# A decode block on one Trainium2 core: the K chunks of a head as an inner loop of two turns, and x's columns in 16 loads

## The chip, the core and the metric

The kernel runs on one core of one Trainium2 chip. The core has a matrix engine (TensorE, PE in the profile; PEld is its weight load), a vector engine (VectorE, DVE), a scalar engine (ScalarE, ACT), GpSimd (POOL) and a sync engine (SyncE, SP). They run separate instruction streams and meet at semaphores. Sixteen DMA engines move data between HBM and the on-chip memory SBUF; in this kernel loads are issued by SP and by ACT, each on a queue of its own (q1 and q10 in the profile). TensorE writes to the banks of PSUM. The metric is the device time of one execution in microseconds, lower is better.

## The reference, cut to what matters

One token goes through layernorm, grouped-query attention over a cache of 65536 positions (8 KV heads, 4 query heads each, head size 128), a residual, a second layernorm and a bilinear gated feed-forward layer with its residual.

```python
q = (layernorm(x) @ wq).reshape(B, Sq, 32, 128)          # x is [1, 1, 512]
scores = einsum("bhqd,bhkd->bhqk", q, k) * (128 ** -0.5)  # k_cache, v_cache: [1, 8, 65536, 128]
o = einsum("bhqk,bhkd->bhqd", softmax(scores), v)
h = x + o.reshape(B, Sq, 4096) @ wo
n = layernorm(h)
out = h + ((n @ w_gate) * (n @ w_up)) @ w_down            # 512 -> 1792 -> 512
```

All data are float32. The two caches are 512 MiB together and are read once.

## The kernel before, in words

**Tiling.** Of each head, K is read in NT = 4 chunks and then V in 4 chunks. A chunk is a tile of 128 partitions x 16384 floats, 64 KB in a partition, 8 MiB in all. Two buffers, `kv[0]` and `kv[1]`, take the chunks in turn. The loads are `sp.dma_start` at line 148 (line 144 for the last V chunk of the last head, which comes in four pieces). Before each load but the first two, SP waits (line 133) until TensorE has finished the chunk that stood in the same buffer, by a count on TensorE's semaphore `pe`. A head's projection weights (`wqo`, lines 138 and 140) are loaded between V chunks. At the end come the weights of the feed-forward layer (lines 154 to 161).

**Start.** ACT issues the load of `x_col`, x as 128 partitions x 4 columns (line 125), then that of `x_row`, x as one row (line 126). SP issues the first head's query weights `wq_sb` (line 128) and the first two K chunks. VectorE sums `x_col` (line 185) after waiting for it at line 184; mean, variance and the normalised `xn` follow, with two small matmuls of TensorE (lines 327 and 330) and a square root on ACT (line 196) between. VectorE then makes small constants (lines 204 to 215) and copies `x_row` (line 218). All of this is in one order on VectorE, ahead of the first head's work.

**TensorE's loop over heads** (line 392, eight turns, code in `head()`). First 16 matmuls make the head's four queries (line 337); VectorE copies them into `q_pad` (line 228) and gives one count on the semaphore `tok`. Then, for each of the four K chunks, TensorE takes the chunk's load off `s_kv` and issues 32 matmuls (line 347) into PSUM bank `psc[s % 2]`. ACT copies the bank out (line 225), VectorE takes a maximum of the copy (line 231); the maxima of chunks 0 and 1 give a count on `tok` each, and chunks 2 and 3 take one before they overwrite the bank. The softmax follows (lines 353 to 365), then the matmuls over the V chunks (line 375) and the output projection (lines 382 and 388).

The loop exists for TensorE alone: the streams of the other engines are written out for all eight heads. `take(s, n)` waits until semaphore `s` has `n` and takes them off.

Of the kernel before, what the change touches and what calls it, by code (L numbers as in the profile page):

```python
# [26 lines left out]
HKV, REP, DH = 8, 4, 128  # L27
SK = 65536
CK = 16384
NT = SK // CK  # L30
# [8 lines left out]
PE_ONLY = bass.OrderedEngineSet([mybir.EngineType.PE])  # L39
# [20 lines left out]
def body(nc, xc, xr, kT, v, wq0, wqo, wo7, wg, wu, wd, out):  # L60
    pe_e, dve_e, act_e, pool_e, sp = nc.tensor, nc.vector, nc.scalar, nc.gpsimd, nc.sync

    def tile(name, *shape, align=32):
        return nc.alloc_sbuf_tensor(name, list(shape), F32, align_bytes=align).ap()

    def bank(name):
        return nc.alloc_psum_tensor(name, [P, 512], F32).ap()

    x_col, x_row = tile("x_col", P, KT), tile("x_row", 1, D)
# [4 lines left out]
    q_pad = tile("q_pad", P, 2 * 28 + REP)  # L74
# [6 lines left out]
    kv = [tile(f"kv{i}", P, CK, align=1024) for i in range(2)]  # L81
# [16 lines left out]
    psc = [bank(f"psc{i}") for i in range(2)]  # L98
    ptp = [bank(f"ptp{i}") for i in range(2)]
    pva, attn = bank("pva"), bank("attn")  # L100
    sm = [bank(f"sm{i}") for i in range(2)]
# [3 lines left out]
    def sem(name):  # L105
        sems.append(nc.alloc_semaphore(name))
        return sems[-1]

    pe, dve, act, pool = (Counter(sem(n)) for n in ("pe", "dve", "act", "pool"))
    tok, atok = sem("tok"), sem("atok")  # L110
    s_kv = [sem("s_kv0"), sem("s_kv1")]
# [5 lines left out]
    s_x, s_xr, s_out = sem("s_x"), sem("s_xr"), sem("s_out")  # L117
# [3 lines left out]
    def pe_at(h, m):  # L121
        return M_HEAD * h + m


    act_e.dma_start(x_col, xc).then_inc(s_x, 16)
    act_e.dma_start(x_row, xr).then_inc(s_xr, 16)

    sp.dma_start(wq_sb, wq0).then_inc(s_wq, 16)
# [45 lines left out]
    def dve_self():  # L174
        dve_e.wait_ge(dve.sem, dve.n)
# [5 lines left out]
    dve.tick(dve_e.memset(mean_m, 1.0 / D))  # L181
    dve.tick(dve_e.memset(ones, 1.0))
    dve.tick(dve_e.memset(eps_t, EPS))
    dve_e.wait_ge(s_x, 16)
    c_s1 = dve.tick(dve_e.tensor_reduce(out=ln_s, in_=x_col, axis=AX.X, op=ALU.add))
    dve_e.wait_ge(pre, PRE_PM)
    dve.tick(dve_e.tensor_copy(ln_m, sm[0][:, 0:1]))
# [33 lines left out]
    for h in range(HKV):  # L221
        copies = []
        for s in range(NT):
            act_e.wait_ge(pe.sem, pe_at(h, M_K + s))
            copies.append(act.tick(act_e.copy(sc[s], psc[s % 2])))  # L225

        dve_e.wait_ge(pe.sem, pe_at(h, M_Q))
        dve_e.tensor_copy(q_pad[:, 28:28 + REP], sm[0][:, 0:REP]).then_inc(tok, 1)
        for s in range(NT):
            dve_e.wait_ge(act.sem, copies[s])  # L230
            i = dve_e.tensor_reduce(out=mx[:, s:s + 1], in_=sc[s], axis=AX.X, op=ALU.max)  # L231
            if s < 2:

                i.then_inc(tok, 1)
            else:
                dve.tick(i)
        dve_self()
        dve_e.tensor_reduce(out=m1, in_=mx, axis=AX.X, op=ALU.max).then_inc(tok, 1)
        dve_e.wait_ge(pe.sem, pe_at(h, M_MX))
        dve.tick(dve_e.tensor_reduce(  # L240
            out=mrow, in_=sm[1][0:1, 0:P].rearrange("p (g h) -> p h g", h=REP), axis=AX.X, op=ALU.max))
        dve_self()
        dve_e.tensor_copy(mexp, mrow.unsqueeze(1).to_broadcast([1, 32, REP])).then_inc(tok, 1)
        dve_e.wait_ge(pe.sem, pe_at(h, M_MB))
        c_bias = dve.tick(dve_e.tensor_scalar(  # L245
            out=nbias, in0=sm[0][:, 0:1], scalar1=-SCALE, scalar2=None, op0=ALU.mult))

        act_e.wait_ge(dve.sem, c_bias)
        for s in range(NT):
            act_e.activation(  # L250
                sc[s], sc[s], AF.Exp, bias=nbias[:, 0:1], scale=SCALE,
                accum_out=sums[:, s:s + 1]).then_inc(atok, 1)
        for s in range(NT):
            dve_e.wait_ge(pe.sem, pe_at(h, M_T + s))
            dve_e.tensor_copy(  # L255
                pt[s].rearrange("p g b h -> p b g h"),
                ptp[s % 2].rearrange("p (b g h) -> p b g h", b=4, h=REP)).then_inc(tok, 1)
        dve.tick(dve_e.tensor_reduce(out=l1, in_=sums, axis=AX.X, op=ALU.add))
        dve_self()
        dve_e.tensor_scalar(  # L260
            out=l4, in0=sel_h, scalar1=l1[:, 0:1], scalar2=None, op0=ALU.mult).then_inc(tok, 1)
        dve_e.wait_ge(pe.sem, pe_at(h, M_L))
        dve.tick(dve_e.reciprocal(linv, sm[1][:, 0:REP]))
        dve_e.wait_ge(pe.sem, pe_at(h, M_V + NT - 1))
        dve_e.tensor_copy(orow, pva).then_inc(tok, 1)  # L265
        dve_self()
        dve_e.wait_ge(pe.sem, pe_at(h, M_PO))
        dve_e.tensor_tensor(
            out=o_pad[:, :, 0], in0=sm[0][:, 0:REP], in1=linv, op=ALU.mult).then_inc(tok, 1)
        if h < LAST:  # L270
            dve_e.wait_ge(dve.sem, c_acc)
            dve_e.wait_ge(pe.sem, pe_at(h, M_AT))
            c_acc = dve.tick(dve_e.tensor_tensor(out=acc, in0=attn, in1=acc, op=ALU.add))
# [47 lines left out]
    mm = pe_e.matmul  # L321

    def take(s, n=1):
        pe_e.wait_ge(s, n).then_inc(s, -n)  # L324
# [9 lines left out]
    def head():  # L334
        for r in range(REP):
            for k in range(KT):
                i = mm(sm[0][:, r:r + 1], wq_sb[:, k, r * P:(r + 1) * P], xn[:, k:k + 1],  # L337
                       start=(k == 0), stop=(k == KT - 1))
        i.then_inc(pe.sem, 1)
        take(tok)  # L340
        for s in range(NT):
            take(s_kv[s % 2], 16)
            if s >= 2:
                take(tok)
            for rs in range(8):
                for j in range(4):
                    i = mm(psc[s % 2][32 * j:32 * j + 32, :],  # L347
                           q_pad[:, 28 - 4 * rs:60 - 4 * rs],
                           kv[s % 2][:, (4 * rs + j) * 512:(4 * rs + j + 1) * 512],
                           start=(rs == 0), stop=(rs == 7))  # L350
            i.then_inc(pe.sem, 1)
        take(tok)
        pe_e.transpose(sm[1][0:1, 0:P], m1, ident).then_inc(pe.sem, 1)  # L353
        take(tok)
        mm(sm[0][:, 0:1], mexp.rearrange("p g h -> p (g h)"), ones[0:1, 0:1],  # L355
           start=True, stop=True).then_inc(pe.sem, 1)
        for s in range(NT):
            take(atok)
            if s >= 2:
                take(tok)  # L360
            for b in range(4):
                i = pe_e.transpose(ptp[s % 2][:, b * P:(b + 1) * P], sc[s][:, b * P:(b + 1) * P], ident)  # L362
            i.then_inc(pe.sem, 1)
        take(tok, 3)
        mm(sm[1][:, 0:REP], ones, l4, start=True, stop=True).then_inc(pe.sem, 1)  # L365
        for j in range(4):
            mm(pva[32 * j:32 * j + 32, :], zeros[:, 0:32], zeros, start=True, stop=False)  # L367
        for n in range(NT):
            vt = kv[n % 2]
            pieces = list(zip(V_CUTS, V_CUTS[1:])) if n == NT - 1 else [(0, 32)]  # L370
            for p, (lo, hi) in enumerate(pieces):
                take(s_vp[p] if len(pieces) > 1 else s_kv[n % 2], 16)
                for w in range(lo, hi):
                    rs, j = divmod(w, 4)
                    i = mm(pva[32 * j:32 * j + 16, :],  # L375
                           pt[n][:, 8 * j + rs, :, :].rearrange("p b h -> p (b h)"),
                           vt[:, w * 512:(w + 1) * 512],
                           start=False, stop=(n == NT - 1 and rs == 7))
            i.then_inc(pe.sem, 1)
        take(tok)  # L380
        for b in range(4):
            i = mm(sm[0][:, 0:REP], orow[:, b * P:(b + 1) * P], sel_b[:, 4 * b:4 * b + 4],  # L382
                   start=(b == 0), stop=(b == 3))
        i.then_inc(pe.sem, 1)
        take(s_w, 16)
        take(tok)
        for r in range(REP):
            i = mm(attn[32 * r:32 * r + 32, :], o_pad[:, r, :], wo_sb[:, r, :],  # L388
                   start=True, stop=True)
        i.then_inc(pe.sem, 1)  # L390

    with nc.Fori(0, HKV, engines=PE_ONLY, hint_back_edge=True):
        head()
# [27 lines left out]
    for b in range(2):  # L421
        i = mm(sm[0][:, 4 * b:4 * b + 4], f_sb[:, b * P:(b + 1) * P], sel_q,
               start=(b == 0), stop=(b == 1))
# [4 lines left out]
    for i in range(2):  # L428
        i2 = mm(sm[1][64 * i:64 * i + 64, 4:6], f_sb[:, 3 * P:FJ], sel_q[:, 2 * i:2 * i + 2],
                start=False, stop=True)  # L430
    i2.then_inc(pe.sem, 1)
    pe_e.wait_ge(dve.sem, c_fp0)
    for c in range(NC):
# [4 lines left out]
        for j in range(4):  # L438
            o = c * D + j * P
            i = mm(pva[32 * j:32 * j + 32, 0:P], f_pad[:, c, :], wd_t[:, o:o + P],  # L440
                   start=False, stop=(c == NC - 1))
# [43 lines left out]
```

## Time and profile before

| | |
|---|---|
| median of 3 runs | 1310.22 us (1310.11 to 1310.87) |
| the profiled execution | 1310.07 us, of which the span from first to last instruction 1308.8 us |
| bytes read from HBM | 564.66 MB |
| TensorE matmul busy | 711.7 us, 54% of the span |
| VectorE, ACT, GpSimd busy | 73.3, 47.2 and 2.5 us |
| DMA queue q1 (SP's loads) | 12248 packets, 564.67 MB |
| DMA queue q10 (ACT's loads) | 146 packets |

The page puts an engine's busy time next to the span; a share of the DMA queues is a share of the 16 DMA engines' time. The timeline view gives start and length in us from the span's start, the engine, the line, the operation and what it writes and reads; in brackets stand the engine's idle time before it and what ended that. An "SPq" or "ACTq" row is the issuing of a load by that engine's sequencer, not the transfer.

### The profile page before, as it was taken

How to read it: one execution, taken by the hardware profiler on the slowest of the kernel's cores; microseconds unless marked ns; L12 is line 12 of the kernel's file. 1: busy time of each engine (PE TensorE's matmuls, PEld its weight loads, DVE VectorE, ACT ScalarE, POOL GpSimd, SP SyncE). 2: the span in 40 equal slices, each digit the busy share in tenths (PEclk: the TensorE clock that was granted, in tenths of full speed). 3: DMA queues.
4: the chain of work that ended last, by engine and by line, in shares of the span. 5: the costliest groups of instructions: out<-in, count | busy, mean ns of one | idle time of the engine just before them, and what ended most of it. 6: DMA issues, size and time to landing. Idle time of an engine off the chain costs nothing. (4 is left out here: it accounts for less than half of the span.)

```text
span 1308.8 us, 10526 instructions
## 1 busy us (share of the span) xinstructions
PE 711.7 (54%) x4922; PEld 247.5 (19%) x4922; DVE 73.3 (6%) x180; ACT 47.2 (4%) x102; POOL 2.5 (0%) x13
## 2 busy tenths in 40 slices
PE   4366384553755446563564636636365465655556
PEld 3012031210312112120131202202021121311113
DVE  0000000100001000010000100001000010000101
ACT  0000000100001000010000100001000010000100
POOL 0000000000000000000000000000000000000000
PEclk9776666776767867767767867678677677687778
DMA  9999999999999999999999999999999999999998
GB/s 417 417 445 429 435 437 431 441 429 441 425 441 425 441 431 437 435 435 435 433 439 427 441 425 441 431 439 433 435 433 435 441 416 450 425 441 429 441 417 373
DMA packets 12404, 564.80 MB, mean 432 GB/s; under 512 B 1509, under 2 KB 1513, under 8 KB 2154
## 3 DMA queue, kind: packets, MB, share of 16 engines
q1 hardware_dynamic: 12248, 564.67, 99.7%
q8 instruction: 6, 0.10, 0.0%
q10 hardware_dynamic: 146, 0.00, 0.0%
q14 instruction: 4, 0.03, 0.0%
HBM read 564.66 MB, written 0.00 MB: 431 GB/s over the span
## 5 line engine op out<-in xcount | busy, mean ns | idle before, releaser
L347 PE MATMUL psc<-kv,q_pad 128*32 128x512 f32 x2048 | 295.2, 741 | 254.0 <-PEq L324 254.0
L375 PE MATMUL pva<-kv,pt 128*16 128x512 f32 x2048 | 280.6, 709 | 276.5 <-PEq L324 276.5
L347 PEld LDWEIGHTS psc<-kv,q_pad 128*32 128x32 f32 x2048 | 81.1, 133 | 461.6 <-issue 461.6
L375 PEld LDWEIGHTS pva<-kv,pt 128*16 128x16 f32 x2048 | 67.5, 111 | 492.4 <-issue 492.4
L225 ACT COPY sc<-psc 128x512 f32<-128x512 f32 x32 | 18.7, 585 | 1142.7 <-PE psc L347 1142.7
L231 DVE TENSOR_REDUCE mx<-sc 128x1 f32<-128x512 f32 x32 | 21.9, 686 | 536.6 <-ACT sc L225 536.6
L337 PEld LDWEIGHTS sm<-xn,wqo_sb 128*128 128x128 f32 x256 | 49.0, 299 | 10.3 <-issue 10.3
L337 PE MATMUL sm<-xn,wqo_sb 128*128 128x1 f32 x256 | 49.7, 329 | 2.2 <-issue 2.2
L265 DVE COPY orow<-pva 128x512 f32<-128x512 f32 x8 | 5.5, 692 | 566.9 <-PE pva L375 566.9
L362 PE MATMUL ptp<-ident,sc 128*128 128x128 f32 x128 | 29.3, 396 | 10.2 <-PEq L324 9.7
L362 PEld LDWEIGHTS ptp<-ident,sc 128*128 128x128 f32 x128 | 21.4, 202 | 15.5 <-issue 14.7
L250 ACT ACTIVATE sc<-sc,nbias 128x512 f32<-128x512 f32 x32 | 22.7, 711 | 20.2 <-DVE nbias L245 20.2
L255 DVE COPY pt<-ptp 128x512 f32<-128x512 f32 x32 | 22.1, 692 | 21.6 <-PE ptp L362 21.6
L367 PE MATMUL pva<-zeros 128*32 128x512 f32 x64 | 12.9, 890 | 0.0
L388 PE MATMUL attn<-wqo_sb,o_pad 128*32 128x512 f32 x64 | 10.8, 748 | 3.4 <-PEq L324 3.4
L382 PE MATMUL sm<-sel_b,orow 128*128 128x4 f32 x64 | 8.2, 252 | 7.2 <-PEq L324 7.2
L382 PEld LDWEIGHTS sm<-sel_b,orow 128*128 128x128 f32 x64 | 7.7, 191 | 14.4 <-issue 14.4
L353 PE MATMUL sm<-ident,m 128*1 128x128 f32 x8 | 2.2, 269 | 13.6 <-PEq L324 13.6
L410 PE MATMUL psc<-kv,hn_pad 128*32 128x448 f32 x64 | 8.2, 654 | 1.8 <-DMA kv<-in_wu 1.0
L365 PE MATMUL sm<-l,ones 128*128 128x4 f32 x16 | 3.9, 312 | 9.6 <-PEq L324 9.6
L355 PE MATMUL sm<-ones,mexp 1*128 1x1 f32 x16 | 3.3, 275 | 5.7 <-PEq L324 5.7
L250 ACT ACTIVATION_READ_ACCUMULATOR sc<-sc,nbias 128x1 f32 x32 | 6.0, 187 | 0.0
(83 smaller groups left out, 64.5 us busy)
## 6 DMA issues: line engine op xcount, KB each, us to landing
wqo_sb<-in_wqo SPq DMA_DIRECT2D x7, 2048.0 KB, 15.1
kv<-in_v SPq DMA_DIRECT2D x1, 4096.0 KB, 21.6
kv<-in_wg SPq DMA_DIRECT2D x1, 3584.0 KB, 18.8
kv<-in_v SPq DMA_DIRECT2D x1, 2048.0 KB, 26.1
kv<-in_v SPq DMA_DIRECT2D x2, 1024.0 KB, 29.1
kv<-in_wu SPq DMA_DIRECT2D x1, 1792.0 KB, 22.9
kv<-in_wu SPq DMA_DIRECT2D x2, 896.0 KB, 25.4
kv<-in_wd SPq DMA_DIRECT2D x1, 1536.0 KB, 19.7
```

Source lines behind the costliest of these rows:

```text
L225: copies.append(act.tick(act_e.copy(sc[s], psc[s % 2])))
L231: i = dve_e.tensor_reduce(out=mx[:, s:s + 1], in_=sc[s], axis=AX.X, op=ALU.max)
L250: act_e.activation(sc[s], sc[s], AF.Exp, bias=nbias[:, 0:1], scale=SCALE, accum_out=sums[:, s:s + 1]).then_inc(atok, 1)
L255: dve_e.tensor_copy(pt[s].rearrange("p g b h -> p b g h"), ptp[s % 2].rearrange("p (b g h) -> p b g h", b=4, h=REP)).then_inc(tok, 1)
L337: i = mm(sm[0][:, r:r + 1], wq_sb[:, k, r * P:(r + 1) * P], xn[:, k:k + 1], start=(k == 0), stop=(k == KT - 1))
L347: i = mm(psc[s % 2][32 * j:32 * j + 32, :], q_pad[:, 28 - 4 * rs:60 - 4 * rs], kv[s % 2][:, (4 * rs + j) * 512:(4 * rs + j + 1) * 512], st ...
L362: i = pe_e.transpose(ptp[s % 2][:, b * P:(b + 1) * P], sc[s][:, b * P:(b + 1) * P], ident)
L367: mm(pva[32 * j:32 * j + 32, :], zeros[:, 0:32], zeros, start=True, stop=False)
L375: i = mm(pva[32 * j:32 * j + 16, :], pt[n][:, 8 * j + rs, :, :].rearrange("p b h -> p (b h)"), vt[:, w * 512:(w + 1) * 512], start=False, ...
L382: i = mm(sm[0][:, 0:REP], orow[:, b * P:(b + 1) * P], sel_b[:, 4 * b:4 * b + 4], start=(b == 0), stop=(b == 3))
L388: i = mm(attn[32 * r:32 * r + 32, :], o_pad[:, r, :], wo_sb[:, r, :], start=True, stop=True)
L410: i = mm(acc[32 * j:32 * j + 32, :FJ], hn_pad[:, k, :], w[:, o:o + FJ], start=(k == 0), stop=(k == KT - 1))
```

## The change

Two things are edited.

**TensorE's K chunks.** The Python loop that wrote out four chunks becomes a hardware loop on TensorE of `NT // 2 = 2` turns inside the loop over heads, whose body holds two chunks, one for each buffer. As both turns run the same code, every chunk now takes a count of `tok`, the first two as well; VectorE's copy into `q_pad` therefore gives 3 counts in place of 1.

**x's columns.** The one load of 128 rows becomes 16 loads on ACT's queue, of 8, 1, 2, 3, ... and 15 rows (8 + 120 = 128). VectorE waits for all of them. The load of `x_row` is issued after them.

```diff
-    act_e.dma_start(x_col, xc).then_inc(s_x, 16)
+    at = 0
+    for r in (8, *range(1, 16)):
+        act_e.dma_start(x_col[at:at + r], xc[at:at + r]).then_inc(s_x, 16)
+        at += r
     act_e.dma_start(x_row, xr).then_inc(s_xr, 16)
...
-    dve_e.wait_ge(s_x, 16)
+    dve_e.wait_ge(s_x, 16 * 16)
...
-        dve_e.tensor_copy(q_pad[:, 28:28 + REP], sm[0][:, 0:REP]).then_inc(tok, 1)
+        dve_e.tensor_copy(q_pad[:, 28:28 + REP], sm[0][:, 0:REP]).then_inc(tok, 3)
...
-        for s in range(NT):
-            take(s_kv[s % 2], 16)
-            if s >= 2:
+        with nc.Fori(0, NT // 2, engines=PE_ONLY):
+            for s in range(2):
+                take(s_kv[s], 16)
                 take(tok)
-            for rs in range(8):
-                for j in range(4):
-                    i = mm(psc[s % 2][32 * j:32 * j + 32, :],
+                for rs in range(8):
+                    for j in range(4):
+                        i = mm(psc[s][32 * j:32 * j + 32, :],
...
-            i.then_inc(pe.sem, 1)
+                i.then_inc(pe.sem, 1)
```

ACT's stream at its start, the loads of x and the square root of the first layernorm; before:

```order
L125 DMA x_col<-in_xc 128x4 [waits barrier_Pool_Activation_PE_DVE_SP_release]
L126 DMA x_row<-in_xr 1x512
L196 ACT_TABLE_LOAD
L196 ACTIVATE ln_t<-sm,eps_t 128x1 [waits pre]
L225 COPY sc<-psc 128x512 [waits pe] x4
```

And now, the last eight of the 16 loads and what follows them (the lines are those of the changed file):

```order
L128 DMA x_col<-in_xc 8x4
L128 DMA x_col<-in_xc 9x4
L128 DMA x_col<-in_xc 10x4
L128 DMA x_col<-in_xc 11x4
L128 DMA x_col<-in_xc 12x4
L128 DMA x_col<-in_xc 13x4
L128 DMA x_col<-in_xc 14x4
L128 DMA x_col<-in_xc 15x4
L130 DMA x_row<-in_xr 1x512
L200 ACT_TABLE_LOAD
L200 ACTIVATE ln_t<-sm,eps_t 128x1 [waits pre]
```

The load of `x_row` and the square root stand behind sixteen loads where they stood behind one.

TensorE's stream in `head()`, from the queries to the first step of the softmax; before:

```order
L337 MATMUL sm0<-xn,wqo_sb 128x1 x16
L347 MATMUL psc0<-kv0,q_pad 32x512 [waits tok,s_kv0]
L347 MATMUL psc0<-kv0,q_pad 32x512 x31
L347 MATMUL psc1<-kv1,q_pad 32x512 [waits s_kv1]
L347 MATMUL psc1<-kv1,q_pad 32x512 x31
L347 MATMUL psc0<-kv0,q_pad 32x512 [waits s_kv0,tok]
L347 MATMUL psc0<-kv0,q_pad 32x512 x31
L347 MATMUL psc1<-kv1,q_pad 32x512 [waits s_kv1,tok]
L347 MATMUL psc1<-kv1,q_pad 32x512 x31
L353 MATMUL sm1<-ident,m1 1x128 [waits tok]
```

And now:

```order
L343 MATMUL sm0<-xn,wqo_sb 128x1 x16
L347 UNCONDITIONAL_BRANCH [waits tok]
L353 MATMUL psc0<-kv0,q_pad 32x512 [waits s_kv0,tok]
L353 MATMUL psc0<-kv0,q_pad 32x512 x31
L353 MATMUL psc1<-kv1,q_pad 32x512 [waits s_kv1,tok]
L353 MATMUL psc1<-kv1,q_pad 32x512 x31
L347 REGISTER_ALU
L347 COMPARE_AND_BRANCH
L359 MATMUL sm1<-ident,m1 1x128 [waits tok]
```

The matmuls of two chunks are written once and run twice, in the same order as before; a branch stands ahead of them, and a register step and a branch behind them.

More of the change, by code (lines that the diff above doesn't have):

```diff
@@ L340, in head @@
         take(tok)
-        for s in range(NT):
-            take(s_kv[s % 2], 16)
-            if s >= 2:
+        with nc.Fori(0, NT // 2, engines=PE_ONLY):
+            for s in range(2):
+                take(s_kv[s], 16)
                 take(tok)
-            for rs in range(8):
-                for j in range(4):
[L347 to L350, printed above, removed]
-            i.then_inc(pe.sem, 1)
+                for rs in range(8):
+                    for j in range(4):
+                        i = mm(psc[s][32 * j:32 * j + 32, :],
+                               q_pad[:, 28 - 4 * rs:60 - 4 * rs],
+                               kv[s][:, (4 * rs + j) * 512:(4 * rs + j + 1) * 512],
+                               start=(rs == 0), stop=(rs == 7))
+                i.then_inc(pe.sem, 1)
         take(tok)
```

## The prediction

> **What bounds the kernel now.** I read the page first: the busy row, the DMA row by slices and the DMA queues.
>
> ```profile
> PE 711.7 (54%) x4922; PEld 247.5 (19%) x4922; DVE 73.3 (6%) x180; ACT 47.2 (4%) x102; POOL 2.5 (0%) x13
> DMA  9999999999999999999999999999999999999998
> q1 hardware_dynamic: 12248, 564.67, 99.7%
> q8 instruction: 6, 0.10, 0.0%
> q10 hardware_dynamic: 146, 0.00, 0.0%
> ```
>
> No compute engine is near its limit, and SP's queue q1 fills 99.7% of the 16 DMA engines' time from the first slice to the last. The kernel ends when its bytes have come. A change can therefore cost time only where q1 runs empty, or where an engine moves more, and it can gain next to nothing.
>
> Whether q1 runs empty is decided by the moment at which TensorE frees a buffer, compared with the end of the load in flight. The timeline shows this at the start, for TensorE and for SP's issues:
>
> ```profile
> 10.77 6.98 PE L337 MATMUL sm<-xn,wqo_sb 128*128 128x1 f32 x32 [2.19 <-issue]
> 25.60 8.82 PE L347 MATMUL psc<-kv,q_pad 128*32 128x512 f32 x64 [7.86 <-PEq L324]
> 45.80 8.96 PE L347 MATMUL psc<-kv,q_pad 128*32 128x512 f32 x64 [11.38 <-PEq L324]
> 65.26 9.47 PE L347 MATMUL psc<-kv,q_pad 128*32 128x512 f32 x64 [10.50 <-PEq L324]
> 34.48 20.66 SPq L148 DMA_DIRECT2D kv<-in_kT  x2
> ```
>
> K0, K1 and K2 land at 25.6, 45.8 and 65.3 us; TensorE needs 9 us for each and waits about 10. K0 is done at 34.4, so the load of K2 is issued at 34.48, with 11 us of K1 still to come. That margin is what the change can spend.
>
> **The inner loop.** It moves no matmul: the order of TensorE's 128 K matmuls per head, the buffers and the counts that SP waits for are the same. A head's takes of `tok` up to the fourth chunk are five, one for the queries and one for each chunk, and five counts serve them: 3 from the queries' copy and one from each of the first two maxima; so the third and fourth chunk still wait for those maxima, as before. Added are a branch at the entry, and a register step with a branch after each turn. The trace shows such a pair only at the end of a head, where it jumps back over the whole body:
>
> ```profile
> 179.07 1.70 PE L388 MATMUL attn<-wqo_sb,o_pad 128*32 128x512 f32 x8 [0.43 <-PEq L324]
> 180.70 6.99 PE L337 MATMUL sm<-xn,wqo_sb 128*128 128x1 f32 x32
> 188.19 9.44 PE L347 MATMUL psc<-kv,q_pad 128*32 128x512 f32 x64 [0.50 <-PEq L324]
> 224.91 1.94 PE L347 MATMUL psc<-kv,q_pad 128*32 128x512 f32 x8 [10.11 <-PEq L324]
> 197.69 0.33 SPq L148 DMA_DIRECT2D kv<-in_kT  x1
> ```
>
> The next head's first matmul starts at 180.70, before the last one of the old head has ended (179.07 + 1.70 = 180.77): that jump costs TensorE nothing that can be seen. The inner loop's jump back carries no prefetch hint, so I bound it by 0 below and by a fetch of code above. Even that would take no more than a few us (wq's 1 MB lands 5.3 us after its issue, quoted below), and the jump stands between K1 and K2, where TensorE idles 10.1 to 10.5 us for the transfer. I take 0; were that cover gone, eight jumps at 5.3 us would be 42 us of TensorE time.
>
> **x's columns.** This is where the time goes. First, what ACT's issues cost and when x arrived:
>
> ```profile
> 0.73 0.41 ACTq L125 DMA_DIRECT2D x_col<-in_xc  x1
> 1.17 0.55 ACTq L126 DMA_DIRECT2D x_row<-in_xr  x1
> 6.23 0.16 DVE L185 TENSOR_REDUCE ln_s<-x_col 128x1 f32<-128x4 f32 x1 [5.08 <-DMA x_col<-in_xc]
> wqo_sb<-in_wq SPq DMA_DIRECT2D x1, 1024.0 KB, 5.3
> x_col<-in_xc ACTq DMA_DIRECT2D x1, 2.0 KB, 5.5
> ```
>
> Issues follow each other at 0.44 to 0.55 us, so the sixteenth is issued at 0.73 + 15 x 0.5 = 8.2 us, 7.5 us later than the only one now. Issuing alone would be harmless: VectorE's sum (T for short) would move from 6.23 to about 8.2 + 5.5 = 13.7 us, and I show below that T may slip to 21.
>
> But from 5.5 us on the DMA engines are full of K. I looked at the packets by queue in short windows, first 3.12 to 3.43 us, then 2.4 to 5.7, then 6 to 43:
>
> ```profile
> q1 hardware_dynamic: 16, 0.13, 103.2%
> q10 hardware_dynamic: 16, 0.00, 2.9%
> ...
> q1 hardware_dynamic: 153, 1.98, 146.5%
> q10 hardware_dynamic: 146, 0.00, 2.6%
> ...
> q1 hardware_dynamic: 256, 15.73, 98.2%
> ```
>
> In 0.31 us each of the 16 engines moved one 8 KB packet of wq (0.13 MB / 16) and one 16-byte packet of x: **the two queues alternate, packet by packet**. All 146 packets of q10 passed in 3.3 us because wq's packets are short. x's 128 rows and x_row's one are 129; the other 17 are completions, 16 for the 128-row load and one for the one-row load. So a load of 128 rows uses 16 engines with 8 rows and a completion each (9 turns), and a load of one row uses one engine with two turns.
>
> In 6 to 43 us a packet is a whole row of K: 15.73 MB / 65536 = 240 rows and 16 completions. A turn of q1 takes 37 x 16 x 0.982 / 240 = 2.42 us. If alternation holds for these, each x packet behind another on its engine waits 2.42 us instead of 0.31.
>
> How many packets of x stand on the busiest engine is not shown for loads of 2 to 15 rows. Lower bound: all evenly spread, (128 rows + 128 completions) / 16 = 16. Upper bound: all of every load on one engine, 128 + 16 = 144. I take **one row and one completion on each of r engines, always counted from the first engine: 32 packets** on the first, as the one-row load puts both its packets on one engine and nothing carries over from one load to the next. With x_row it is 34. By 5.5 us about 9 have passed (the 9 turns of x_col in the same time), 25 are left. K0 and K1 offer 2 x (8 rows + 1 completion) = 18 turns; then q1 is empty, because K2 cannot be issued before K0 is consumed, and the remaining 7 pass at once. So x is complete when K1 is, whatever the exact count above 18: **T = 45.8 us**, the moment at which K1 lands today.
>
> The Trainium skill ("DMA: Bandwidth & Descriptors", on why a DMA increments its semaphore by 16) says that such a load uses the largest number of engines up to 16 that divides its row count, and that these are the lowest-numbered ones. It agrees with the 16 + 1 completions here, and by it the first engine has just those 32 packets. The same page (section on queues, rings and completion order) lets an engine drain some 9 to 17 descriptors of one queue before it switches; the 16 and 16 packets above speak against that, and what it would give is the first rival.
>
> **The sum.** From T, VectorE's and TensorE's steps to the first query matmul took 10.77 - 6.23 = 4.54 us; x_row is there by then as well. From the first query matmul to the issue of the load that reuses K0's buffer, with K0 already there, head 1 needs 197.69 - 180.70 = 16.99 us. So K2 is issued at 45.8 + 4.5 + 17.0 = 67.3 us instead of 34.48. It meets empty queues: wq took 5.3 us, of which 8 x 0.31 = 2.5 moved data, so 2.8 us are latency; K2 lands after 2.8 + 8 x 2.42 = 22.2 us, at 89.5 instead of 65.3. **That is 24.2 us late.** K1 is consumed by 67.3 + 9.5 = 77, well before 89.5, so q1 does not run empty again, and the rest follows as it does now, shifted. Nothing can catch up on a queue that is full to the end: 1310.07 + 24.2 = 1334.3 for the profiled execution, 0.15 more against the median of 1310.22. I say **1334 us**.
>
> The margin that this uses up: K2 would have to be issued by 65.3 - 22.2 = 43.1 us to arrive in time, so T may be as late as 43.1 - 21.5 = **21.6 us** without any loss.
>
> **The rivals.**
>
> 1. *x slips through.* If x's packets need not wait for a whole 64 KB row each (several pass in one turn, as that rule of the Trainium skill has it, or rows are cut for the arbitration), T is about 13.7, under the point of 21.6 that decides, and the time stays at **1310**. For it: no row shows x beside 64 KB packets. Against it: the strict one to one beside 8 KB packets. Chance 0.15. This is the case on the other side.
> 2. *x waits, but less.* If a row and its completion pass in one turn, some 5 loads are through by 5.5 us, the other 11 need 11 x 2.42 = 27 us, T is 32.5 and the loss 11: **1321**. If loads are spread evenly, the 16 packets per engine, 14 of them after 5.5 us since the large loads are issued last, give T = 39.4 and a loss of 18: **1328**. Against the first: in 3.3 us 146 packets needed turns of their own, completions included. Chance 0.15.
> 3. *The inner loop fetches its code again at every jump.* Packets of q8 would then ride on an engine that has no time to spare. A 16 KB packet is a quarter of a row, 0.6 us; two blocks for each of eight jumps are 16 x 0.6 = 10 us on top: **1344**. The Trainium skill ("Runtime: NRT & Kernel Launch", instruction fetch) states this danger: a taken branch out of the two pages held forces a fetch. The six packets of q8 in the whole run speak against it: the jump over the whole head was taken seven times, and in 170 to 1280 us, where all but the first of them lie, q8 has no row at all, in the window's answer:
>
> ```profile
> q1 hardware_dynamic: 9489, 481.42, 100.1%
> q14 instruction: 3, 0.02, 0.0%
> ```
>
> Chance 0.06.
>
> **How the numbers follow.** Forecast 0.62, rivals 0.15, 0.15 and 0.06, and 0.02 for a gain I can't name. The forecast's own range is 1330 to 1338: T can lie 1.5 us either side, as the engines end K1 at different times, and the latency and TensorE's pace in K0 (8.8 to 9.5 us) add as much. The range reaches down to 1319 for the second rival and up to 1345 for the third; only the first and the unnamed gain are left out, 0.17. A measurement here can tell about 0.2%, 2.6 us, from no change. Slower: 0.62 + 0.15 + 0.06 = 0.83; same 0.15; faster 0.02.
>
> **What would show it.** Right: VectorE's sum of x_col starts near 46 us and waits for the DMA; TensorE's first query matmul is near 50, K0 and K1 run back to back up to about 77, and SP issues K2 near 67; the DMA share has a hole of about 22 us between 45 and 69 and none later; q10 has 128 + 128 + 2 = 258 packets, a few of them in each 2.4 us up to 45. Rival 1 shows T below 21 and no hole, rival 2 a T of 32 to 40, rival 3 more than six q8 packets. I am wrong in kind if the hole lies elsewhere, or if time is lost with no hole.

## The result, and the profile after

The change makes the kernel slower: 1334.87 us median (1334.26 to 1335.27, 6 runs) against 1310.16 us (1309.9 to 1310.87, 6 runs) before, a ratio of 1.0188 with a 95% interval of 1.0178 to 1.0198. The profiled execution took 1334.44 us, its span 1333.1 us.

The page of the kernel after: busy times, the DMA row by slices and the DMA queues.

```profile
PE 714.5 (54%) x4922; PEld 247.9 (19%) x4922; DVE 73.3 (6%) x180; ACT 47.3 (4%) x102; POOL 2.5 (0%) x13
DMA  9299999999999999999999999999999999999998
q1 hardware_dynamic: 12248, 564.67, 97.9%
q8 instruction: 5, 0.08, 0.0%
q10 hardware_dynamic: 258, 0.00, 0.0%
```

The work is the same: as many matmuls, as many packets and bytes on q1. What is new is one bad slice out of 40, the second (a slice is 33 us), and 258 packets on q10 in place of 146. Everything behind that slice is as full as before.

The timeline of the kernel after shows the slice from inside: ACT's issues, VectorE's sum of x_col, TensorE's matmuls (L343 queries, L353 K chunks) and SP's issue of K2.

```profile
0.73 6.37 ACTq L128 DMA_DIRECT2D x_col<-in_xc  x16
45.31 0.16 DVE L189 TENSOR_REDUCE ln_s<-x_col 128x1 f32<-128x4 f32 x1 [44.17 <-DMA x_col<-in_xc]
49.86 6.98 PE L343 MATMUL sm<-xn,wqo_sb 128*128 128x1 f32 x32 [2.19 <-issue]
57.69 15.27 PE L353 MATMUL psc<-kv,q_pad 128*32 128x512 f32 x128 [0.85 <-PEq L330]
66.15 0.33 SPq L152 DMA_DIRECT2D kv<-in_kT  x1
88.36 8.43 PE L353 MATMUL psc<-kv,q_pad 128*32 128x512 f32 x64 [15.40 <-PEq L330]
```

ACT is done with issuing at 7.1 us, yet x_col is complete only at 45.3, 39 us later than before. The first query matmul starts at 49.9, and K0 and K1, both long landed, are consumed in one piece of 15.3 us. K2 is issued at 66.15 instead of 34.48 and starts on TensorE at 88.36 instead of 65.26.

The windows view of the kernel after (window, its length, busy time and count for PE, PEld, DVE, ACT and POOL, TensorE's granted clock, DMA share, GB/s) shows what the DMA engines do meanwhile:

```profile
24.00:44.00 20.00, 0.00 (x0) 0.00 (x0) 0.00 (x0) 0.00 (x0) 0.00 (x0) 1.00 0.97 420
44.00:67.00 23.00, 17.43 (x112) 10.82 (x116) 2.99 (x16) 0.85 (x2) 0.00 (x0) 1.00 0.00 1
67.00:87.00 20.00, 5.96 (x56) 1.61 (x48) 1.15 (x2) 0.59 (x1) 0.00 (x0) 0.76 1.00 423
```

For 23 us, from the end of K1 to K2's first bytes, q1 and q10 move nothing; the 1 GB/s is one 16 KB packet of code on q8. That is the time that was lost.

### The profile page after: what moved, and what is told of

It reads as the page before. It is cut to its first block, busy times and chain, and to the rows that moved or that the text cites. A ratio compares the mean times of both kernels' runs of the same rounds, so it can differ in the third digit from the quotient of the medians.

```text
span 1333.1 us, 10605 instructions
## 1 busy us (share of the span) xinstructions
PE 714.5 (54%) x4922; PEld 247.9 (19%) x4922; DVE 73.3 (6%) x180; ACT 47.3 (4%) x102; POOL 2.5 (0%) x13
## 5 line engine op out<-in xcount | busy, mean ns | idle before, releaser
L381 PE MATMUL pva<-kv,pt 128*16 128x512 f32 x2048 | 284.1, 716 | 270.1 <-PEq L330 270.1
L353 PE MATMUL psc<-kv,q_pad 128*32 128x512 f32 x2048 | 292.8, 736 | 243.0 <-PEq L330 243.0
L353 PEld LDWEIGHTS psc<-kv,q_pad 128*32 128x32 f32 x2048 | 80.6, 132 | 448.6 <-issue 448.6
L343 PEld LDWEIGHTS sm<-xn,wqo_sb 128*128 128x128 f32 x256 | 49.2, 299 | 10.2 <-issue 10.2
L343 PE MATMUL sm<-xn,wqo_sb 128*128 128x1 f32 x256 | 49.9, 329 | 2.2 <-issue 2.2
L368 PEld LDWEIGHTS ptp<-ident,sc 128*128 128x128 f32 x128 | 21.7, 203 | 15.3 <-issue 14.8
L261 DVE COPY pt<-ptp 128x512 f32<-128x512 f32 x32 | 22.1, 692 | 21.6 <-PE ptp L368 21.6
```

Source lines behind the costliest of these rows:

```text
L261: dve_e.tensor_copy(pt[s].rearrange("p g b h -> p b g h"), ptp[s % 2].rearrange("p (b g h) -> p b g h", b=4, h=REP)).then_inc(tok, 1)
L353: i = mm(psc[s][32 * j:32 * j + 32, :], q_pad[:, 28 - 4 * rs:60 - 4 * rs], kv[s][:, (4 * rs + j) * 512:(4 * rs + j + 1) * 512], start=(rs ...
L381: i = mm(pva[32 * j:32 * j + 16, :], pt[n][:, 8 * j + rs, :, :].rearrange("p b h -> p (b h)"), vt[:, w * 512:(w + 1) * 512], start=False, ...
```

## The experiments

In all of them the computation is whole. Each ran beside the kernel before on the same chip.

**Which half of the change does it.** First the inner loop alone, with x's old load:

```diff
-    at = 0
-    for r in (8, *range(1, 16)):
-        act_e.dma_start(x_col[at:at + r], xc[at:at + r]).then_inc(s_x, 16)
-        at += r
+    act_e.dma_start(x_col, xc).then_inc(s_x, 16)
...
-    dve_e.wait_ge(s_x, 16 * 16)
+    dve_e.wait_ge(s_x, 16)
```

> The inner loop with x's one load of 128 rows. Theory (all of the loss is x's packets waiting behind rows of K, the loop costs nothing): VectorE's sum of x_col starts near 6.2 us, K2 is issued near 34.5, no hole in the DMA share, 1310 us within 0.2%. Rival (the loop costs TensorE time or code fetches that reach the end): more than 1313 us, with more packets on q8 than the 6 of before.

Measured: 1309.88 us against 1310.04, a ratio of 1.0 (0.9991 to 1.0009). From this kernel's page, and from its timeline in head 1:

```profile
q8 instruction: 5, 0.08, 0.0%
...
180.37 6.99 PE L340 MATMUL sm<-xn,wqo_sb 128*128 128x1 f32 x32
188.17 9.13 PE L350 MATMUL psc<-kv,q_pad 128*32 128x512 f32 x64 [0.81 <-PEq L327]
205.30 9.10 PE L350 MATMUL psc<-kv,q_pad 128*32 128x512 f32 x64 [8.00 <-PEq L327]
224.60 5.82 PE L350 MATMUL psc<-kv,q_pad 128*32 128x512 f32 x28 [10.21 <-PEq L327]
```

In this head the gap between the queries and K0 is 0.81 us where it was 0.50, so the loop's entry takes about 0.3 us. TensorE still has 8 and 10 us of waiting in front of K1 and K2, and the code comes in 5 packets of q8, one fewer than before. The loop costs nothing at the end.

Then the other half, the 16 loads with the four chunks written out (the first two hunks of the change's diff alone):

> The 16 loads with the four chunks written out as before. Theory: the whole loss, 1334 to 1335 us, with the sum of x_col at 45 us and a hole of 23 us. Rival (loop and loads together make the loss, since the loop's entry waits in the first head): under 1330 us.

Measured: 1335.18 us, ratio 1.0195 (1.018 to 1.0211), the sum of x_col at 45.23 us. The loads carry the whole loss.

**What about the loads.** Sixteen loads in place of one are more issues, more completions, and more packets on the engine that takes the first row of each. Two loads take away the first two of these and keep the third:

```diff
-    for r in (8, *range(1, 16)):
+    for r in (127, 1):
...
-    dve_e.wait_ge(s_x, 16 * 16)
+    dve_e.wait_ge(s_x, 16 * 2)
```

> The changed kernel with two loads of x_col, of 127 and of 1 row, in place of 16. Theory (what counts is the number of packets on the busiest DMA engine, and 127 rows have no share that divides by more than one, so 128 packets stand on the first engine): the sum of x_col near 45 us, as K1 ends, 1334 to 1336 us. Rival (the number of loads or of completions is what costs): x by about 8 us and 1310 us. Should 127 rows be spread over several engines all the same, q10 has more than 127 + 1 + 1 + 1 + 2 = 132 packets.

Measured: 1334.93 us, ratio 1.0192 (1.0176 to 1.0207), as slow as the sixteen. The packets of q10 over the whole run (the page of this kernel), and then those of q1 and q10 between 7 and 43 us:

```profile
q10 hardware_dynamic: 132, 0.00, 0.0%
...
q1 hardware_dynamic: 256, 15.73, 100.8%
q10 hardware_dynamic: 16, 0.00, 0.0%
```

132 packets are 127 + 1 + 1 rows and one completion for each of three loads, so each load ran on one engine: 127 rows went to a single one. That engine takes a sixteenth of the 256 packets of q1 in this window, 16, and beside them pass 16 packets of x. **One for one, beside 64 KB rows.** The sum of x_col starts at 45.03 us. Two loads with one completion each cost as much as sixteen, so neither the number of loads nor that of completions is the cost by itself.

**How many turns.** With 16 rows in each load every engine gets one row and one completion of each. The diff is as above, with `[16] * 8` and `16 * 8`, and for the second run with `[64] * 2` and `16 * 2`.

> The changed kernel with 8 loads of 16 rows. Every engine then has 8 rows and 8 completions of x. Theory (one packet passes for each packet of q1; two to four pass before K's rows start at 5 us): 12 to 14 turns of which one falls on a completion of K0, the sum of x_col at 33 to 38 us, a loss of 11 to 17 us, 1321 to 1327 us. Rival 1 (a row and its completion pass in one turn): 6 turns, the sum at 18 to 21 us, no loss, 1310. Rival 2 (x waits until q1 is empty, whatever its count): 45 us and 1334.

> The changed kernel with 2 loads of 64 rows. Every engine has 8 rows and 2 completions, 10 packets, one more than with one load. Theory: the second load's 5 packets pass by 5.1 + 5 x 2.42 = 17 us at the latest, the sum of x_col lies between 6.5 and 19 us, under the point of about 22 from which time is lost, 1310 us within 0.2%. Rival (any x packet that is still to come at 5 us costs its turn at the end): up to 12 us more.

Measured: 1327.33 us, ratio 1.0133 (1.0117 to 1.0148), and 1309.94 us, ratio 0.9999 (0.999 to 1.0009). VectorE's sum in these two kernels' timelines:

```profile
36.99 0.16 DVE L189 TENSOR_REDUCE ln_s<-x_col 128x1 f32<-128x4 f32 x1 [35.84 <-DMA x_col<-in_xc]
...
18.05 0.16 DVE L189 TENSOR_REDUCE ln_s<-x_col 128x1 f32<-128x4 f32 x1 [16.91 <-DMA x_col<-in_xc]
```

With 8 loads x ends well before K1 does, so x does not wait for an empty queue; and it ends far later than 7 turns would take, so a row and its completion do not share a turn. The upper end of my expectation for the time was missed by 0.3 us, because the point from which time is lost lies a little earlier than I had it (below). Two loads of 64 rows delay the sum by 12 us and cost nothing, since that still lies under the point.

**The price of a turn.** If x waits for one packet of q1 each time, shorter packets make it wait less. K0 and K1 are cut into CUT loads of columns, so that their rows are 32 KB or 16 KB:

```diff
-                sp.dma_start(kv[buf], src).then_inc(s_vp[0] if whole else s_kv[buf], 16)
+                if h == 0 and i < 2:
+                    for c in range(CUT):
+                        cs = slice(c * CK // CUT, (c + 1) * CK // CUT)
+                        sp.dma_start(kv[buf][:, cs], src[:, cs]).then_inc(s_kp[buf], 16)
+                else:
+                    sp.dma_start(kv[buf], src).then_inc(s_vp[0] if whole else s_kv[buf], 16)
...
+    for i in range(2):
+        pool_e.wait_ge(s_kp[i], 16 * CUT)
+        pool_e.sem_inc(s_kv[i], 16)
```

> The changed kernel with K0 and K1 each loaded as 2 loads of half the columns, so that a row of q1 is 32 KB and takes 1.21 us; GpSimd, otherwise idle, counts the pieces and passes K0 and K1 on to TensorE. Theory (a packet of x waits for one packet of q1, so the price of a turn is the length of q1's rows): 28 turns are left on the first engine at 5 us, of 8 x 1.21 / 9 = 1.08 us on average, the sum of x_col near 36 us, a loss of 14 to 16 us, 1324 to 1327 us. Rival (x waits until q1 is empty): 45 us and 1334.

> The same with 4 loads of a quarter of the columns, rows of 16 KB and 0.61 us. Theory: 28 turns of 0.54 us, the sum of x_col at 21 to 22 us, just at the point from which time is lost, 1310 to 1312 us. Rival (x waits until q1 is empty): 45 us and 1334.

Measured: 1325.56 us, ratio 1.0119 (1.0101 to 1.0137), with halves and 1311.51 us, ratio 1.0013 (1.0003 to 1.0023), with quarters. The sum of x_col, first with halves, then with quarters:

```profile
35.72 0.16 DVE L199 TENSOR_REDUCE ln_s<-x_col 128x1 f32<-128x4 f32 x1 [34.57 <-DMA x_col<-in_xc]
...
20.70 0.16 DVE L199 TENSOR_REDUCE ln_s<-x_col 128x1 f32<-128x4 f32 x1 [19.56 <-DMA x_col<-in_xc]
```

The same 16 loads of x and the same bytes of K give 45.3, 35.7 and 20.7 us for rows of 64, 32 and 16 KB. The 36 and 21 to 22 us expected came from 28 turns times the length of a row (the second was missed by 0.3 us). With halves K0 and K1 offer 2 x 2 x (8 rows + 1 completion) = 36 turns, more than x needs, so the end of K1 no longer cuts the wait short, and the count on the busiest engine shows: were the loads spread evenly, some 14 turns would be left and the sum would come near 5 + 14 x 1.08 = 20 us.

**What ends the wait.** SP holds back K1, K0, or everything until x_col is there; the first is

```diff
             buf = len(done) % 2
+            if h == 0 and i == 1:
+                sp.wait_ge(s_x, 16 * 16)
```

the second has `i == 0`, and in the third the wait stands ahead of wq's load.

> The changed kernel, but SP issues K1 only when all 16 loads of x_col have landed. q1 then holds only K0. Theory (what is left of x passes at once when q1 runs empty): the sum of x_col near 25.5 us, when K0 has landed, a hole of about 3 us there and one of up to 2 us before K2, 1313 to 1316 us. Rival (x's own 256 packets take 40 us, or cost by themselves what was seen): the sum near 45 us, K1 issued after it and more than 1334 us.

> The changed kernel, but SP issues K0 only when all 16 loads of x_col have landed; wq is issued as before, so x stands beside 8 KB packets alone. The theory (x waits behind long rows of q1) gives the sum of x_col at 8 to 10 us, K0 issued then and landing 22 us later near 31, 6 to 8 us late, 1316 to 1318 us. What it is to tell apart: in the changed kernel no packet of x passed between 2 and 5 us beside wq. If rows of K0 queued behind wq keep x out, more than 60 packets of q10 now pass between 2 and 5 us; if wq's own packets do, or if x's loads are slow in coming, it is fewer than 20.

> The changed kernel, but SP issues nothing, wq included, until all 16 loads of x_col have landed, so x has the DMA engines to itself. Theory (16 loads are not slow by themselves): the sum of x_col at 8 to 9.5 us, about 2 us after the last of ACT's issues, and every transfer then 7.5 to 9 us later than in the kernel before, 1317 to 1320 us. Rival (the loads of a few rows are slow by themselves): the sum above 15 us and more than 1324 us.

Measured, in this order: 1316.34 us, ratio 1.0047 (1.0029 to 1.0065); 1315.06 us, ratio 1.0037 (1.0023 to 1.0051); 1316.81 us, ratio 1.005 (1.0034 to 1.0067). The three sums of x_col:

```profile
26.90 0.16 DVE L191 TENSOR_REDUCE ln_s<-x_col 128x1 f32<-128x4 f32 x1 [25.76 <-DMA x_col<-in_xc]
...
8.19 0.16 DVE L191 TENSOR_REDUCE ln_s<-x_col 128x1 f32<-128x4 f32 x1 [7.05 <-DMA x_col<-in_xc]
...
7.74 0.16 DVE L190 TENSOR_REDUCE ln_s<-x_col 128x1 f32<-128x4 f32 x1 [6.59 <-DMA x_col<-in_xc]
```

With K0 alone queued x is complete 1.4 us later than I had it, when K0 ends. With the engines to itself it needs 7.7 us, which is ACT's issuing, up to 6.6 us in that run, and 1.1 us more. So 16 small loads are not slow; they are slow behind K. Holding all of K back until they are through costs 5 to 7 us, less than the 25 that the change costs, and both of these ways are slower than the kernel before, as was to be expected of a queue that has no idle time to give. All three times missed what I had expected by a little: 0.3 us above the range with K1 held, 0.9 us below it with K0 held and 0.2 us below it with all held; the sum of the last came 0.3 us before the earliest I had given.

The last two kernels' packets of q10 between 2 and 5 us, first with K0 held, where wq runs alone beside x, then with all held:

```profile
q1 hardware_dynamic: 122, 0.93, 75.0%
q10 hardware_dynamic: 12, 0.00, 0.2%
...
q10 hardware_dynamic: 90, 0.00, 1.5%
```

Twelve, fewer than the 20 that I had set as the mark: it is not K0's rows, queued behind wq, that keep x's later loads out in these 3 us; they stay out beside wq as well. All twelve fall between 4.5 and 5 us, as wq ends; from 2 to 4.5 us the run shows no packet of q10.

## Why the prediction was right

1. **The bound.** "A change can therefore cost time only where q1 runs empty": the 24.4 us between the profiled executions are one hole of 23 us and a remainder that point 5 takes up.

2. **The inner loop at 0.** Right, by the inner loop alone. The entry's 0.3 us is hidden behind the waits for K1 and K2. The third rival's code fetches did not come: 5 packets on q8. The two-page rule of the Trainium skill ("Runtime: NRT & Kernel Launch", instruction fetch) finds no support here: the seven outer jumps go back over a whole head, in whose first turn three 16 KB packets of code came, and in 195 to 1280 us, where all seven lie, q8 has no row. The eight inner jumps made no fetch that shows either, but whether they leave two pages no run shows.

3. **Alternation, and T.** Forecast 45.8 us, measured 45.31. "If alternation holds for these" was an extrapolation from 8 KB to 64 KB packets; the loads of 127 and 1 rows show it directly, 16 beside 16 rows of one engine. That T is K1's end because q1 then runs empty is shown by holding K1 back: T follows to K0's end. The choice of one row and one completion per engine, always from the first engine, is borne out in part: 127 rows went to a single engine, 16 to 16 engines, and the runs with shorter rows fit 28 turns on one engine and not 14; that the loads of 2 to 15 rows all begin on the same engine is not visible in the trace itself.

4. **The step that was wrong without harm:** "By 5.5 us about 9 have passed, 25 are left." In the kernel after, from 2 to 5.5 us:

```profile
q1 hardware_dynamic: 148, 2.00, 138.5%
q10 hardware_dynamic: 2, 0.00, 0.0%
```

Two packets passed, on all engines together, besides the first load's 16 before 2 us. I had taken the nine turns of one load issued together with wq for what later loads would get. The forecast survived because anything above 18 gives the same T; the expectations for the later runs used the corrected count.

5. **The sum.** The steps behind T held, row by row: 49.86 - 45.31 = 4.55 us (4.54 forecast), 66.15 - 49.86 = 16.29 (16.99; TensorE's granted clock was 1.00 in this window and 0.75 during K0 of head 1), 88.36 - 66.15 = 22.2 (22.2). K2 was then 23.1 us late, not 24.2, but the end was 24.4 us late. So it is luck in part that the forecast of 24.2 for the end came out within 0.2 us: two differences of about 1 us cancel. The margin was also smaller than forecast. With each kernel's profiled execution, to which its T belongs, against the median of the kernel before, T minus the loss is 21.0 us in the kernel after (45.31 - 24.28), 20.4 with 8 loads of 16 rows, 20.6 with halves and 20.1 with quarters, where I had 21.6. I had measured K2's lateness at the last of the 16 engines. Completions of K2 stand in the DMA rows as packets under 512 B; the kernel before from 62.5 to 63.4 us and from 63.9 to 65.5, then the kernel after from 86 to 87.3:

```profile
DMA packets 20, 0.66 MB, mean 728 GB/s; under 512 B 10, under 2 KB 10, under 8 KB 10
DMA packets 5, 0.26 MB, mean 164 GB/s; under 512 B 1, under 2 KB 1, under 8 KB 1
...
DMA packets 18, 0.59 MB, mean 454 GB/s; under 512 B 9, under 2 KB 9, under 8 KB 9
```

Before, ten engines have finished K2 by 63.4, and one comes alone after 63.9. After, nine have by 87.3. The middle engine is some 24 us late, only the straggler less. So the hole took up the straggler's delay once, and the engines drifted apart again later; this reading fits the rows, no run was made for it.

6. **The rivals.** "x slips through" falls with the 16 beside 16, and with it the rule that an engine drains 9 to 17 descriptors before it switches (Trainium skill, "DMA: Bandwidth & Descriptors", on queues, rings and completion order): beside long rows it took one packet at a time here. "A row and its completion pass in one turn" falls with the 8 loads of 16 rows, which needed 37 us and not 21. The loads spread evenly, the second half of that rival, fall with a T of 45.31 in place of 39.4 and with the sum at 35.7 us with halves.

## What to carry to other kernels

A small load that is issued on another queue behind bulk loads waited here, at each of its packets on the busiest DMA engine, for a whole packet of the bulk queue, with rows of 64, 32 and 16 KB; count its rows and completions there and multiply by the time of a bulk row, until the bulk queue runs empty. So let a small tensor that gates the start come in one load whose rows spread over all 16 engines, issued before or with the first bulk load, and compare its arrival with the moment at which the bulk queue would run dry. In this kernel, whose DMA queue is full, rolling TensorE's K chunks into a loop cost nothing, because TensorE's waits of 8 to 10 us are longer than the 0.3 us of the loop's entry; other loops were not tried.

## What the runs showed of the hardware that was not expected

The loads of x that ACT issued after its first, some 0.4 us apart (16 issues in 6.37 us), did not alternate with wq's 8 KB packets: in the kernel after no packet of x passed between 2 and 5 us, and with K0 held back 12, though the one load of the kernel before, issued in the same moment as wq, alternated packet by packet. The moment of the issue alone does not decide it: with two loads of 64 rows the first, issued with wq, shows no packet between 2 and 4.5 us and all its 80 (64 rows, 16 completions) between 4.5 and 5.5. Why these loads are kept out there, and yet get their turn beside 64 KB rows, stays open.

Expected before its run, but easily overlooked: a 127-row load stood on one DMA engine with all its rows, 132 packets of q10 in all. It has one row fewer than the load of 128, and x arrived 39 us later.
